# Zero products on TensorE at the start, another order for the second pair's reads, and weight bits rounded on ScalarE

## The chip, the cores and the metric

One NeuronCore of a Trainium2 chip runs the whole kernel. The metric is device time in microseconds (us) of one execution, the median of several. Below, PE is TensorE (PEld its weight loads), DVE is VectorE, ACT is ScalarE, POOL is GpSimd and SP is the engine that issues most DMAs.

## The reference

```
# q, k, v: (4, 8, 576, 64); M_prev: (4, 8, 64, 64); z_prev: (4, 8, 64); beta: (8,)
scores = scale * q @ k^T, causal mask;  a = softmax(scores);  local = a @ v
q_p = phi(q)                       # phi(x) = x + 1 for x > 0, else exp(x)
mem_out = (q_p @ M_prev) / (q_p @ z_prev + 1e-6)
g = sigmoid(beta)
x = g * mem_out + (1 - g) * local  # as a (2304, 512) matrix of tokens
out = (silu(x @ w_gate) * (x @ w_val)) @ w_out    # 512 -> 1536 -> 512
```

All in float32 at the accuracy of float32: operands are cut into a high and a low part (float32r), and a product is three matmuls (high x high, high x low, low x high).

## The kernel before

**Two stages, one program per engine.** Helpers named `pe`, `act`, `dve` and `pool` keep the order of the source on their engine, so the position of a line in the loop is its position in that engine's queue. Every such instruction has line L84 in the profile; the tiles' names tell them apart. Instructions written `ACT.`, `DVE.`, `POOL.` or `SP.` are placed by the framework's scheduler. The helper `rot` hands out a fixed number of buffers of a name in turn.

**Stage one, attention.** 16 pairs of heads run through a loop of 17 rounds (`n` from 0 to `NP` = 16). In round n the pair `cur` makes its scores on PE (`scores` for the query tiles t = 0 to 3, tiles `s`; `scores4` for the last 64 queries of both heads), DVE reads them with mask and row extreme (the `reads`), ACT takes the exponential (`exp`), and POOL multiplies by row weight and gate (`weighed`, tiles `ps`, `pl`, `p`). The pair before, `old`, is transposed on PE (`turned1`, `turned`, tiles `tr`), multiplied with its values (`values`), and its memory part is read (`recall`: PE products `tr<-mm,ph` of the feature map `ph` with the memory `mm`, then `w` and `mem` on DVE). `give` cuts the result into `xh` and `xl` and stores it. The next pair is split into high and low on POOL (`after.split`, `after.lows`: `qh`, `kh`, `ql`, `kl`). Round 0 also makes the gates (`gates`: `one_less` for the local part `og`, `memory_gates` for `gx`) and both feature maps of the first two pairs (`phi0`, `phi`).

**Weights.** Each of the 12 slices of 128 hidden columns has three thirds (gate, value, out), listed in `thirds`. They arrive as 64-bit words (`raw_load`, tile `wraw`) and are put together from the upper half (`raw_top`, an ACT Prelu into `we`, then `third_clamp`) and three low bits (`third_move`, into `wa` or `wr`: a shift on DVE for the first four, an arithmetic rounding of one byte on POOL for the others), which `third_word` joins on DVE. Slices 0 to 2 are cut into high and low (`wgh`, `wgl`, `woh`, `wol`, the low parts in `low_part`). The first four thirds are worked during rounds 2 to 16 (`EARLY`).

**Stage two, the gated feed-forward part.** It takes three blocks of 768 tokens by 12 slices, 36 units. The first three units (`eight`) are four products of 12 matmuls with 384 columns; the others (`seven`) have seven products of six (a Strassen form), for which the token sums `xr`, `xt`, `xm` and their parts `xp3` to `xp7` (`sums`, `spreads`) and the weight sums `tt` (`operands`) are made on DVE and ACT. From the second unit on, the unit before gives 18 matmuls with 512 columns (`lower`, `woh`/`wol` with `uh`/`ul`). Two PSUM banks take the products in turn. In the first block `third` is called three times in each unit for the slices to come; the list `plan` says after which product each such piece of work is put into the queues.

Of the kernel before, what the change touches and what calls it, by code (L numbers as in the profile page):

```python
# [9 lines left out]
F32 = mybir.dt.float32  # L10
F32R = mybir.dt.float32r
I32 = mybir.dt.int32
U8 = mybir.dt.uint8
AF = mybir.ActivationFunctionType
# [30 lines left out]
def attention_moe(ctx: ExitStack, tc: tile.TileContext, qt, kt_, v, m, beta, wg, wv, wo, out):  # L45
# [49 lines left out]
    def rot(pool, name, shape, dtype, n):  # L95
        held = slots.setdefault(name, [0, []])
        if len(held[1]) < n:
            held[1].append(pool.tile(shape, dtype, name=f"{name}{len(held[1])}"))
        held[0] += 1
        return held[1][(held[0] - 1) % n]  # L100
# [8 lines left out]
    def split_lo(dst, src, hi, kind=""):  # L109
        eng = pool if kind in ON_POOL else dve  # L110
        return eng.tensor_tensor(dst, src, hi.bitcast(F32), op=ALU.subtract)

    ident = const.tile([128, 128], F32, name="ident")
    make_identity(nc, ident)
    warm = const.tile([128, 1], F32, name="warm")
    DVE.memset(warm, 0.0)
    ACT.activation(warm, warm, AF.Exp)
    maskp = const.tile([128, 512], F32, name="maskp")
    POOL.memset(maskp, 0.0)
    POOL.affine_select(  # L120
# [39 lines left out]
    xs = {p: [near.tile([128, 2, N2], F32R, name=f"x{p}{part}") for part in "hl"] for p in ("p1", "p2", "p7", "p4")}  # L160

    held, wout, wr = {}, {}, {}
    thirds = [(0, 0), (0, 1), (0, 2), (1, 0)]
    work_of = [[(1, 1), (3, 0), (3, 1)]]
    work_of += [[(n, 2)] + [(n + 1 + (n >= PLAIN - 1), j) for j in range(2)] for n in range(1, NF - 2)]
    work_of += [[(n, 2)] for n in range(NF - 2, NF)]
    slots_of, at = [], len(thirds)
# [7 lines left out]
    def raw_load(n, after=None):  # L175
        if n < len(thirds):
            f, j = thirds[n]
            raws[n] = rot(wp, "wraw", [128, 512, 2], I32, 4)
            ld = SP.dma_start(raws[n].rearrange("p a b -> p (a b)"), (wg, wv, wo)[j][f].bitcast(I32))
            if after is not None:  # L180
                follow(ld, after, "the loads that the attention waits for go first")

    def raw_top(act, n):
        if n < len(thirds):
            tops[n] = rot(wp, "we", [128, 512], F32, 2)
            act.activation(tops[n], raws[n][:, :, 1].bitcast(F32), AF.Prelu, scale=2.0**-111, alpha=2.0**32)

    def low_part(dve):
# [11 lines left out]
    def third_move(eng, n):  # L200
        f, j = thirds[n]
        if f < PLAIN or j == 2:
            wa[n] = rot(wp, "wa", [128, 512], I32, 3)
        else:
            if j == 0:
                wr[f] = rot(wp, "wr", [128, 1024], F32, 2)
            wa[n] = wr[f][:, j * 512 : j * 512 + 512].bitcast(I32)
        if eng is dve:
            eng.tensor_scalar(wa[n], raws[n][:, :, 0], 29, None, op0=ALU.logical_shift_right)
        else:  # L210
            last_byte = raws[n].rearrange("p a b -> p (a b)").bitcast(U8).rearrange("p (a b) -> p a b", b=8)[:, :, 3]
            eng.tensor_scalar(wa[n], last_byte, 1.0 / 32, 31.0 / 64, op0=ALU.mult, op1=ALU.subtract)

    def third_word(act, dve, n):
        f, j = thirds[n]
# [28 lines left out]
    with tc.tile_pool(name="sb", bufs=1, reuse_waits="tile") as sb:  # L244
# [3 lines left out]
        def pair_load(n):  # L248
            b, pr = divmod(n, NPAIR)
            qr = rot(sb, "qr", [128, 768], F32, NR)  # L250
            kr = rot(sb, "kr", [128, 576], F32, NR)
            for dst, src in ((qr, qt), (kr, kt_)):
                queue = ACT if n == 0 and dst is kr else SP
                loads[n] = queue.dma_start(dst, src[b, pr])
            return qr, kr

        def pair_load_v(n):
# [50 lines left out]
        class Pair:  # L308
# [81 lines left out]
            def exp(self, t, h):  # L390
                c, p = 2 * t + h, self.pts[(t, h)][:, 0 : 128 * (t + 1)]
                act.activation(
                    p, p, AF.Exp, bias=self.mx[:, c : c + 1], scale=-1.0, accum_out=self.sm[:, c : c + 1]
                )
# [137 lines left out]
        for n in range(NP + 1):  # L532
            cur = pairs[n] if n < NP else None
            old = pairs[n - 1] if n > 0 else None
            after = pairs[n + 1] if n + 1 < NP else None
            exp = cur.exp if cur else nothing
            scores = cur.scores if cur else lambda t: nothing
            turned, turned1 = (old.turned, old.turned1) if old else (nothing, nothing)
            if cur:
                cur.begin()  # L540
            if old:
                old.turns()
            low = ending()
            reads = [scores(t) for t in range(2)]
            reads[0](0)
            reads[0](1)
            low()
            if n == 0:
                cur.lows()
            reads[1](0)  # L550
            reads[1](1)
            if after and n:
                after.split()
            exp(0, 0)
            turned1(0, act)
            turned1(1, act)
            exp(0, 1)
            exp(1, 0)
            turned(2, 0, dve)
            turned(2, 1, dve)  # L560
            exp(1, 1)
            scale = old.recall() if old else nothing
            first = lambda: cur.weighed(((0, 0), (0, 1), (1, 0), (1, 1)))
            if n == 0:
                after.split()
                one_less, memory_gates = gates()
                after.lows()
            elif cur:
                first()
            scale()  # L570
            if after and n:
                after.lows()
            if n:
                phi = after.phi_parts() if after else nothing
            reads = [scores(t) for t in range(2, 4)]
            reads[0](0)
            reads[0](1)
            exp(2, 0)
            exp(2, 1)
            turned(3, 0, act)  # L580
            turned(3, 1, dve)
            read4 = cur.scores4() if cur else nothing
            reads[1](0)
            turned(4, 0, act, dve)
            reads[1](1)
            exp(3, 0)
            exp(3, 1)
            if n == 0:
                one_less()
                first()  # L590
            read4()
            if cur:
                cur.exp4()
            if n == 0:
                memory_gates()
                phi0()
                phi = after.phi_parts()
            if old:
                old.recalled()
                old.values()  # L600
            if cur:
                cur.weighed(((2, 0), (2, 1), (3, 0), (3, 1)))
            phi()
            if cur:
                cur.weighed(((4, 0),))
            ending = old.leave() if old else lambda: nothing
            if n + 2 < NP:
                with later_by(P_LOAD):
                    pairs[n + 2].load()
            if after:  # L610
                after.load_v()
            for i, at in enumerate(EARLY):
                if n == at:
                    raw_top(act, i)
                if n == at + 1:
                    third_clamp(dve, i)
                if n == at + (2 if i < 3 else 1):
                    third_move(dve, i)
                if n == at + (3 if i < 3 else 2):
                    third_word(act, dve, i)  # L620
                if n == at + (4 if i < 3 else 2):
                    low_part(dve)
            if n in AHEAD:
                raw_load(AHEAD.index(n), loads.get(n + 2))

        n = len(EARLY)
        raw_load(n + 3)
        raw_top(act, n)
        raw_top(act, n + 1)
        third_clamp(pool, n)  # L630
        third_move(pool, n)
        ending()()

    nj = N2 // 128
    with tc.tile_pool(name="stg2", bufs=1, reuse_waits="tile") as stg2, \
# [220 lines left out]
        for n, unit in enumerate(units):  # L856
# [14 lines left out]
            if n < len(units) - 1 and n + 1 >= PLAIN:  # L871
                ready[n + 1], work = operands(units[n + 1][1])
                if plain:
                    work = [work[0] + work[1], work[2], work[3], work[4] + work[5] + work[6]]
                for k, some_ in enumerate(work):
                    plan[k] += some_
            for k, work in arrive:
# [2 lines left out]
            if plain:  # L880
                if f == 0:
                    _, due, mix = sums(t0, True)
                if f < 2:
                    for k in range(4):
                        plan[k].append(due[4 * f + k])
                if f == 1:
                    plan[2] += spreads(mix, ("h", "p6"))
                    plan[3] += spreads(mix, ("l", "p6"))
                if f == PLAIN - 1:
                    for k, p in ((0, "p5"), (1, "p3")):  # L890
                        plan[k] += spreads(mix, ("h", p))
                        plan[k + 2] += spreads(mix, ("l", p))
                    arrive = [(0, spreads(mix, ("h", "p7"))), (1, spreads(mix, ("l", "p7")))]
            if not end:
                follows = ORDER[ORDER.index(t0) + 1]
# [89 lines left out]
```

## Time and profile before

| | |
|---|---|
| median of 3 runs | 626.1 us (625.47 to 626.37) |
| the profiled execution | 626.68 us |
| its span in the trace | 624.9 us |
| busy: PE, DVE, ACT, POOL | 604.7, 494.7, 383.5, 268.1 us |
| attention until the feed-forward part | about 0 to 194 us |

The span is what the trace covers from the first to the last instruction of the program; the time holds 1.8 us more. PE's busy time counts pipelined matmuls from start to modelled end, so a busy PE can still be waiting in part. Below 1.00, the granted clock (PEclk) says that PE had less than its full 2.4 GHz.

### The profile page before, as it was taken

Reading aid. Unit: us, or ns where it says so; the run is one execution under the profiler, and the core shown is the slowest. Engines: PE = TensorE matmul, PEld = TensorE weight load, DVE = VectorE, ACT = ScalarE, POOL = GpSimd, SP = SyncE. Lnnn points to the kernel's source line nnn. Section 1 sums busy time; section 2 is a strip of 40 time slices with the busy share of each in tenths; the row PEclk is TensorE's granted clock in tenths of the full one; section 3 lists DMA queues with packets and bytes.
Section 4 is the critical chain, followed back from the end, with each engine's and each line's share of the span. In section 5 each row is a group of like instructions: output and inputs, shape, how many; then the busy total and the mean of one; then the engine's idle time right before and its main releaser. Section 6 shows DMA issues by size and latency. Waiting matters only on the chain.

```text
span 624.9 us, 11274 instructions
## 1 busy us (share of the span) xinstructions
PE 604.7 (97%) x3794; PEld 534.9 (86%) x3794; DVE 494.7 (79%) x1209; ACT 383.5 (61%) x892; POOL 268.1 (43%) x282
## 2 busy tenths in 40 slices
PE   5999999999999899999999999999999999999997
PEld 3777788778778798988889999999999999999995
DVE  6799899999986899999999666566788765665653
ACT  6788888888875467666657644455446654454442
POOL 6899999999965986867740000000000000000000
PEclk9799999999999999999999999999999999999999
DMA  8355856757435775799638532232756631332212
GB/s 244 96 157 172 268 163 188 239 161 212 150 100 172 217 238 183 237 294 314 218 135 286 168 117 88 72 128 71 238 172 214 202 102 67 102 102 67 70 33 101
DMA packets 48745, 102.46 MB, mean 164 GB/s; under 512 B 6960, under 2 KB 16176, under 8 KB 48688
## 3 DMA queue, kind: packets, MB, share of 16 engines
q1 hardware_dynamic: 48544, 101.45, 50.1%
q8 instruction: 30, 0.49, 0.3%
q10 hardware_dynamic: 144, 0.29, 0.1%
q14 instruction: 27, 0.22, 0.1%
HBM read 74.99 MB, written 26.74 MB: 163 GB/s over the span
## 4 chain that ended last, share of the span: by engine, by line
PE 80%; DVE 9%; POOL 4%; ACT 3%; issue 2%; DMA 1%; DVEq 0%; POOLq 0%
PE s L84 50%; PE tr L84 30%; ACT pl L84 2%; DVE xr L84 1%; POOL we L84 1%; POOL wa L84 1%; DVE tl L84 1%; POOL wr L84 1%; DVE rs L84 1%; DVE pl L84 1%; DVE mem L84 1%; DMA kr<-in_kt_dram 1%; DVE zh L84 1%; ACT g L84 1%; DVE wa L84 1%
## 5 line engine op out<-in xcount | busy, mean ns | idle before, releaser
L84 POOL TENSOR_SCALAR pl<-pl,rs,og 128x384 f32<-128x384 f32 (+1 forms) x64 | 56.0, 886 | 10.9 <-DVE rs L84 10.9
L84 ACT ACTIVATE zh<-zh 128x384 f32<-128x384 f32 x33 | 17.3, 526 | 70.4 <-DVE zh L84 70.3
L84 PE MATMUL tr<-woh,uh 128*128 128x512 f32 x144 | 57.3, 398 | 0.0
L84 PE MATMUL tr<-wol,uh 128*128 128x512 f32 x144 | 56.7, 394 | 0.0
L84 PE MATMUL tr<-woh,ul 128*128 128x512 f32 x144 | 56.6, 393 | 0.0
L84 DVE TENSOR_TENSOR zv<-s,zv 128x384 f32<-128x384 f32 x33 | 18.3, 556 | 47.7 <-PE s L84 47.5
L84 ACT CAST th<-tt 128x512 fp32r<-128x512 f32 x66 | 41.0, 622 | 18.2 <-DVE tt L84 14.9
L84 ACT ACTIVATE pl<-pl,mx 128x384 f32<-128x384 f32 (+1 forms) x64 | 42.3, 663 | 14.2 <-DVE mx L84 14.2
L84 PE MATMUL tr<-g,vp 128*64 128x320 f32 (+4 forms) x448 | 48.7, 360 | 0.0
L84 DVE TENSOR_TENSOR tl<-tt,th 128x512 fp32r<-128x512 f32 x66 | 46.9, 711 | 0.0
L84 PE MATMUL s<-kh,qh 64*128 64x128 f32 (+4 forms) x160 | 37.6, 389 | 7.4 <-ACT kh L84 5.4
L84 PEld LDWEIGHTS tr<-g,vp 128*64 128x64 f32 x448 | 29.5, 137 | 17.6 <-issue 2.3
L84 POOL TENSOR_SCALAR we<-we 128x512 f32<-128x512 f32 x32 | 30.1, 940 | 28.1 <-ACT we L84 25.8
L84 POOL TENSOR_SCALAR wr<-wraw 128x512 int32<-128x512 uint8 x18 | 38.5, 2136 | 1.4
L84 DVE TENSOR_TENSOR zg<-s,zp 128x384 f32<-128x384 f32 x33 | 18.4, 558 | 25.9 <-ACT bh L84 20.6
L84 DVE CUSTOM_DVE_ANT_0 pl<-s,maskp 128x384 f32<-128x384 f32 (+1 forms) x64 | 38.1, 615 | 0.7 <-PE s L84 0.7
L84 ACT CAST uh<-zh 128x384 fp32r<-128x384 f32 x36 | 18.5, 514 | 29.7 <-DVE zh L84 29.4
L84 DVE TENSOR_TENSOR bl<-wr,bh 128x512 fp32r<-128x512 f32 x66 | 36.5, 553 | 0.0
L84 PE MATMUL tr<-ident,pl 128*128 128x128 f32 x224 | 32.3, 281 | 2.3 <-DVE xl L84 1.6
L84 POOL TENSOR_SCALAR ps<-ps,rs,og 128x128 f32<-128x128 f32 (+1 forms) x64 | 31.9, 511 | 6.0 <-DVE rs L84 5.1
L84 ACT CAST bh<-wr 128x512 fp32r<-128x512 f32 x66 | 33.9, 513 | 0.0
L84 DVE COPY g<-tr 128x384 f32<-128x384 f32 (+1 forms) x64 | 32.0, 519 | 2.1 <-PE tr L84 0.8
(187 smaller groups left out, 2031.6 us busy)
## 6 DMA issues: line engine op xcount, KB each, us to landing
wr<-wdr SPq DMA_DIRECT2D x24, 512.0 KB, 3.3
qr<-in_qt_dram SPq DMA_DIRECT2D x16, 384.0 KB, 3.1
wraw<-in_wg_dram SPq DMA_DIRECT2D x12, 512.0 KB, 4.4
wraw<-in_wv_dram SPq DMA_DIRECT2D x12, 512.0 KB, 4.8
wraw<-in_wo_dram SPq DMA_DIRECT2D x12, 512.0 KB, 4.4
wol<-wdo SPq DMA_DIRECT2D x24, 256.0 KB, 2.8
woh<-wdo SPq DMA_DIRECT2D x24, 256.0 KB, 3.2
vp<-in_v_dram SPq DMA_DIRECT2D x16, 320.0 KB, 4.4
```

The source lines that it names most:

```text
L84: ins = getattr(eng, name)(*args, **kw)
```

## The change

Five things are changed.

- **Zeros on PE.** `spin(n)` issues n float32 products of a zero tile with itself into a bank of the `tr` ring that is not yet in use: eight ahead of everything, one after each of the first two scores of round 0, two before and two after its `scores4`, and three in round 1 after the scores of t = 0 and 1.
- **First loads.** The first pair's q and k come in five pieces on two queues instead of two whole loads.
- **Order in rounds 0 and 1.** The last weighing of pair 0, its feature map (`phi0`) and the memory gates move from the end of round 0 to behind the reads of t = 0 and 1 in round 1 (`late`); the second feature map's DVE part moves from round 0 to the end of round 1.
- **Weights.** For gate and value thirds, the rounding moves from POOL to ACT (an Identity with scale and bias, one byte of the raw word to an integer). The third (1, 1) is begun in the last round, with the joining of the two thirds before stage two, and `we` has three buffers. The Silu table is asked for at the head of the last round.
- **Token sums of the first three units.** The sums and their parts are spread over units 0 and 1 where they went to units 0, 1 and 2.

```diff
+    zero = const.tile([128, 128], F32, name="zero")
+    DVE.memset(zero, 0.0)
+    spare = [rot(psT, "tr", [128, 512], F32, PS_T) for _ in range(PS_T)][-1]
+    def spin(n):
+        for _ in range(n):
+            pe.matmul(spare[:, 0:128], zero, zero, start=True, stop=True)
+    spin(8)
...
+    low_bias = const.tile([128, 1], F32, name="low_bias")
+    DVE.memset(low_bias, -31.0 / 64)
...
-    thirds = [(0, 0), (0, 1), (0, 2), (1, 0)]
-    work_of = [[(1, 1), (3, 0), (3, 1)]]
+    thirds = [(0, 0), (0, 1), (0, 2), (1, 0), (1, 1)]
+    work_of = [[(3, 0), (3, 1)]]
...
-            tops[n] = rot(wp, "we", [128, 512], F32, 2)
+            tops[n] = rot(wp, "we", [128, 512], F32, 3)
...
+        if j == 2:
+            eng.tensor_scalar(wa[n], last_byte, 1.0 / 32, 31.0 / 64, op0=ALU.mult, op1=ALU.subtract)
         else:
-            last_byte = ...
-            eng.tensor_scalar(wa[n], last_byte, 1.0 / 32, 31.0 / 64, op0=ALU.mult, op1=ALU.subtract)
+            act.activation(wa[n], last_byte, AF.Identity, scale=1.0 / 32, bias=low_bias)
...
-            for dst, src in ((qr, qt), (kr, kt_)):
-                queue = ACT if n == 0 and dst is kr else SP
-                loads[n] = queue.dma_start(dst, src[b, pr])
+            if n == 0:
+                for queue, dst, src, c in (
+                    (SP, qr, qt, slice(128, 384)), (ACT, kr, kt_, slice(0, 256)), (SP, qr, qt, slice(384, 768)),
+                    (ACT, kr, kt_, slice(256, 576)), (SP, qr, qt, slice(0, 128)),
+                ):
+                    queue.dma_start(dst[:, c], src[b, pr, :, c])
+            else:
+                for dst, src in ((qr, qt), (kr, kt_)):
+                    loads[n] = SP.dma_start(dst, src[b, pr])
...
+            if n == NP:
+                act.activation(warm, warm, AF.Silu)
             if old:
                 old.turns()
             low = ending()
-            reads = [scores(t) for t in range(2)]
+            reads = []
+            for t in range(2):
+                reads.append(scores(t))
+                if n == 0:
+                    spin(1)
+            if n == 1:
+                spin(3)
...
             reads[1](1)
+            if n == 1:
+                for work in late:
+                    work()
...
             turned(2, 1, dve)
+            if n == NP:
+                for i in range(2):
+                    raw_top(act, len(EARLY) + i)
+                third_clamp(pool, len(EARLY))
+                third_move(pool, len(EARLY))
...
+            if n == 0:
+                spin(2)
             read4 = cur.scores4() if cur else nothing
+            if n == 0:
+                spin(2)
...
             if n == 0:
-                memory_gates()
-                phi0()
-                phi = after.phi_parts()
+                phi1 = after.phi_parts()
+            if n == NP:
+                for i in range(2):
+                    third_word(act, dve, len(EARLY) - 1 + i)
+                    raw_load(len(EARLY) + 3 + i)
...
-            phi()
-            if cur:
-                cur.weighed(((4, 0),))
+            if n == 0:
+                late = [lambda cur=cur: cur.weighed(((4, 0),)), phi0, memory_gates]
+            else:
+                if n == 1:
+                    phi1()
+                phi()
+                if cur:
+                    cur.weighed(((4, 0),))
...
-                if n == at + (3 if i < 3 else 2):
+                if n == at + 3 and i < 3:
                     third_word(act, dve, i)
-                if n == at + (4 if i < 3 else 2):
+                if n == at + 4 and i < 3:
                     low_part(dve)
...
-        n = len(EARLY)
-        raw_load(n + 3)
-        raw_top(act, n)
-        raw_top(act, n + 1)
-        third_clamp(pool, n)
-        third_move(pool, n)
         ending()()
+        low_part(dve)
+        i = len(EARLY) + 1
+        third_clamp(pool, i)
+        third_move(pool, i)
+        raw_top(act, i + 1)
...
-                    work = [work[0] + work[1], work[2], work[3], work[4] + work[5] + work[6]]
+                    work = [work[0] + work[1], work[2] + work[3], work[4] + work[5], work[6]]
...
                 if f == 0:
                     _, due, mix = sums(t0, True)
-                if f < 2:
-                    for k in range(4):
-                        plan[k].append(due[4 * f + k])
+                    for k, some_ in enumerate(((0,), (1,), (2, 4), (3,))):
+                        plan[k] += [due[i] for i in some_]
                 if f == 1:
-                    plan[2] += spreads(mix, ("h", "p6"))
-                    plan[3] += spreads(mix, ("l", "p6"))
+                    for k in range(3):
+                        plan[k].append(due[5 + k])
+                    for k, p in ((0, "p5"), (2, "p6")):
+                        plan[k] += spreads(mix, ("h", p))
+                        plan[k + 1] += spreads(mix, ("l", p))
                 if f == PLAIN - 1:
-                    for k, p in ((0, "p5"), (1, "p3")):
-                        plan[k] += spreads(mix, ("h", p))
-                        plan[k + 2] += spreads(mix, ("l", p))
+                    plan[0] += spreads(mix, ("h", "p3"))
+                    plan[2] += spreads(mix, ("l", "p3"))
```

## Rows read from the trace of the kernel before

**Rows 1.** The page, part 1: busy time of each engine.

```profile
PE 604.7 (97%) x3794; PEld 534.9 (86%) x3794; DVE 494.7 (79%) x1209; ACT 383.5 (61%) x892; POOL 268.1 (43%) x282
```

**Rows 2.** Windows: start:end, length, busy us of each engine, clock, DMA.

```profile
194.00:200.00 6.00, 6.00 (x35) 6.00 (x36) 3.86 (x6) 4.59 (x8) 5.15 (x4) 1.00 0.66 212
...
200.00:216.00 16.00, 13.43 (x72) 12.25 (x71) 13.43 (x17) 6.20 (x12) 15.37 (x9) 1.00 0.67 210
...
216.00:236.00 20.00, 19.77 (x102) 17.83 (x100) 19.67 (x31) 12.58 (x27) 16.39 (x11) 1.00 0.70 219
```

**Rows 3.** The chain that ended last, in order of time: start, us, what.

```profile
12.92 2.53 POOL ps L84 x4
...
28.60 0.88 PE s L84 x12
...
39.82 0.89 PE s L84 x12
...
198.54 2.55 POOL wr L84
...
241.67 1.05 PE s L84 x6
...
242.72 0.69 PE tr L84 x3
```

**Rows 4.** Timeline, first 32 us: start, us, engine, operation, [idle before <-releaser].

```profile
4.83 0.76 ACT L84 CAST kh<-kr 128x256 fp32r<-128x256 f32 x2 [2.18 <-DMA kr<-in_kt_dram]
...
10.02 1.42 POOL L84 TENSOR_TENSOR kl<-kr,kh 128x576 fp32r<-128x576 f32 x1
...
12.92 2.61 POOL L84 TENSOR_SCALAR ps<-ps,rs,og 128x128 f32<-128x128 f32 x4 [1.49 <-DVE rs L84]
...
15.57 3.37 POOL L84 TENSOR_SCALAR pl<-pl,rs,og 128x384 f32<-128x384 f32 x4
...
18.31 2.53 PE L84 MATMUL tr<-mm,ph 128*128 128x130 f32 x10
...
30.78 1.28 PE L84 MATMUL tr<-mm,ph 128*128 128x130 f32 x10
```

**Rows 5.** Timeline of PEld: one weight load of 128 columns, twice.

```profile
10.33 0.33 PEld L84 LDWEIGHTS s<-kl,qh 128*128 128x128 f32 x1
...
23.69 0.19 PEld L84 LDWEIGHTS s<-kl,qh 128*128 128x128 f32 x1
```

**Rows 6.** Windows over PE's slow stretch.

```profile
16.00:22.00 6.00, 5.68 (x26) 4.46 (x26) 4.26 (x19) 3.98 (x12) 5.26 (x8) 0.50 0.20 66
```

**Rows 7.** Timeline of PE, round 16 and the first units.

```profile
186.62 0.52 PE L84 MATMUL tr<-ident,pl 128*128 128x128 f32 x3 [0.43 <-POOL pl L84]
...
193.91 0.44 PE L84 MATMUL s<-xp1h,wgh 128*128 128x384 f32 x1
...
207.47 0.44 PE L84 MATMUL s<-xp1h,wgh 128*128 128x384 f32 x1 [2.11 <-DVE zh L84]
...
230.69 0.34 PE L84 MATMUL s<-xp1h,bh 128*128 128x384 f32 x1
...
236.34 0.44 PE L84 MATMUL s<-xp7l,th 128*128 128x384 f32 x1 [0.56 <-DVE xp7l L84]
```

**Rows 8.** Timeline of ACT, round 16 and the first unit.

```profile
184.30 0.35 ACT L84 CAST xh<-tr 128x256 fp32r<-128x256 f32 x1
...
185.10 0.43 ACT L84 CAST xh<-tr 128x320 fp32r<-128x320 f32 x1 [0.45 <-PE tr L84]
...
195.41 1.28 ACT L84 ACT_TABLE_LOAD   x1
...
198.55 0.67 ACT L84 ACTIVATE we<-wraw 128x512 f32<-128x512 f32 x1
```

**Rows 9.** Timeline of DVE: one form, twice.

```profile
203.03 1.01 DVE L84 TENSOR_TENSOR ul<-zg,uh 128x384 fp32r<-128x384 f32 x1
...
208.20 0.55 DVE L84 TENSOR_TENSOR ul<-zh,uh 128x384 fp32r<-128x384 f32 x1
```

More of the change, by code (lines that the diff above doesn't have):

```diff
@@ L209, in third_move @@
             eng.tensor_scalar(wa[n], raws[n][:, :, 0], 29, None, op0=ALU.logical_shift_right)
-        else:
-            last_byte = raws[n].rearrange("p a b -> p (a b)").bitcast(U8).rearrange("p (a b) -> p a b", b=8)[:, :, 3]
-            eng.tensor_scalar(wa[n], last_byte, 1.0 / 32, 31.0 / 64, op0=ALU.mult, op1=ALU.subtract)
+            return
+        last_byte = raws[n].rearrange("p a b -> p (a b)").bitcast(U8).rearrange("p (a b) -> p a b", b=8)[:, :, 3]
+        if j == 2:
+            eng.tensor_scalar(wa[n], last_byte, 1.0 / 32, 31.0 / 64, op0=ALU.mult, op1=ALU.subtract)
+        else:
+            act.activation(wa[n], last_byte, AF.Identity, scale=1.0 / 32, bias=low_bias)
     def third_word(act, dve, n):
```

## The prediction, made before the change was run

> **What bounds the kernel now.** I read the page first: PE is busy for 604.7 of 624.9 us [rows 1]. So where PE runs at its pace nothing but fewer matmuls helps, and the change takes none away; what can be gained lies where PE waits or is slow. The chain of waits and the windows show two such places.
>
> The first is rounds 0 and 1, up to about 29 us. The chain goes from the first loads (ACT stands idle until the first k lands at 4.83 us) to POOL, whose first four weighings (12.92 us, 2.61 us long) wait for DVE's row weights, and then to PE [rows 3, 4]. PE is slow there in a second sense: between 16 and 22 us the granted clock is 0.50 [rows 6], the lower level of 1.2 GHz, and the ten records of the memory products take 2.53 us where round 2 has them in 1.28 [rows 4]. The windows print 1.00 for the first stretches too, but the durations contradict it: a weight load takes 0.33 us at 10.33 and 0.19 at 23.69 [rows 5]. So PE runs at the lower level from its first product on, rises shortly before 12 us, falls at about 15 after a pause, and rises again at 22.
>
> The second place is the start of stage two, 194 to 236 us. From 194.6 on the chain is made of POOL's clamps and roundings of one third after the other [rows 3] (the piece of 2.55 us stands for them), then of DVE. The windows give POOL 36.9 of these 42 us, DVE 37.0, ACT 23 [rows 2]. PE waits 2.11 us at 207.47 and 0.56 at 236.34, both for DVE [rows 7], which had waited for POOL.
>
> **First period, step by step.** Eight zero products stand ahead. A float32 product of this size is two records; five took 1.28 us in round 2 and 2.53 at the lower level [rows 4], so eight cost 4.0 us at the lower level, from about 1 us to 5. Real data is ready between 4 and 5 us, so they hold PE up by 0 to 0.8 us; I take nothing, because POOL hides it: its first weighing can't start before it has split pair 1, which ends at 11.44 us [rows 4] and rests on pair 1's loads. Their issues move back by two DMA issues on SP; but the bytes ahead of them are the same, and I leave their landing where it was (bounds 0 to +0.8 us).
>
> What the eight buy: PE has been busy before the first score, so the scores should run at 2.4 GHz, and the first pieces of q and k are 256 of 672 KB, so DVE's first subtraction comes up to 1.2 us earlier. Either of the two brings DVE's row weights forward by the 1.2 us that lie between 12.92 and POOL's free time of about 11.7. Term a: **-1.2 us** (bounds: 0, if loads and clock give nothing; -1.4, POOL's limit).
>
> Next is PE's start into the memory products, at 18.31 us. It waits for POOL's first two large weighings (a part of the 3.37 us from 15.57 [rows 4]), which follow by -1.2, and then for six transposes at the lower level, from 17.50; at the higher level these take about 0.4 us less. Term b: **-0.4 us**. The feature map and the gates, now behind the four reads of pair 1 on DVE, would be late next: the reads are ready at about 13.5 us and the late work ends near 17, just ahead of need. Behind the late work on DVE stand the copies of the transposes; their banks are two of four, so PE doesn't wait for these.
>
> From the start of the memory products to the next round's scores it took 18.31 to 28.60, 10.3 us, in round 1, and 30.78 to 39.82, 9.0 us, in round 2 [rows 3, 4]. At the higher level round 1 should take the time of round 2. Term c: **-1.3 us**. The nine other zero products cost 0.26 us each where PE would work, and nothing where it waits; they stand in such waits, and I count nothing (bound +0.5). Together **-2.9 us** (bounds 0 and -3.4). If the clock falls all the same, b and c are gone and -1.2 is left. From round 2 on each round begins when the one before lets it, so the gain is kept.
>
> **Round 16.** The Silu table is now loaded at its head. ACT is free from 184.65 to 185.10, where the cast of 320 columns waits for PE [rows 8]. The load takes 1.28 us and stood alone at 195.41 [rows 8]; with the small instruction behind it ACT is free at about 186.1, so the cast comes 1.0 us later, DVE's low part of it too, and PE's transposes at 186.62 [rows 7], which need that bank, by about 0.5: the subtraction ended shortly before them. Term d: **+0.5 us** (bounds 0 and +1.0). The two Prelus of weights, one rounding and the joinings of thirds 3 and 4 go where ACT and DVE wait for PE later in this round; they would cost 0.6 us more if ACT's copies of the transposes came late by them.
>
> The Trainium skill ("ScalarE: Activation LUTs", What ACT_TABLE_LOAD costs) adds a drain of about 1.38 us to a switch of 1.28. The trace doesn't show it: the load starts at 195.41, and the next ACTIVATE is under way at 196.70. By the page, d would be near +1.9 and the time 622.2; I go by the row.
>
> **Start of stage two.** The pace of PE: six matmuls of 384 columns take 1.05 us, three of 512 columns 0.69 [rows 3]. The first unit is 48 of the first kind, 8.4 us; the second and third have 18 of the other besides, 12.5 us each: 33.5 us in all. They took from 193.91 to 230.69, 36.8 us [rows 7], so 3.3 are lost, and 0.6 in the fourth unit: 3.9 us are all there is to gain.
>
> POOL loses 8 of its 11 roundings in this stretch, 2.55 us each [rows 3]: 20 of 36.9 us, and it no longer sets the pace. ACT gets them. The trace has no Identity from bytes. Its nearest row is the Prelu that reads every second word of the same tile, 0.67 us [rows 8]; the upper bound is POOL's 2.55. I take 0.67, since it is the same engine, the same size and the same stride. ACT then has 23 + 5.4 of 42 us, well below PE.
>
> DVE is next. It worked 37.0 us between 194 and 236 [rows 2], more than PE's 33.5. Beside a rounding on POOL one of its instructions takes 1.01 us that elsewhere takes 0.55 [rows 9], a loss of 0.46; eight roundings less give back at most 3.7 us, and as not each of them met such an instruction I take 2.5. That leaves 34.5 us of DVE, 1.0 more than PE needs, so about 1.0 of the 3.9 us stays lost. The new order of the sums puts DVE's work earlier, where it stood idle (13.43 of 16 us busy between 200 and 216 [rows 2]), so that it can be done in time. Term e: **-2.9 us** (bounds: -3.9, and -0.5 if DVE's queue holds PE up as before).
>
> Later units of the first block have two roundings on ACT each, hidden behind PE.
>
> **The sum.** -2.9 + 0.5 - 2.9 = -5.3 us. The profiled execution took 626.7 us, 0.6 over the median of 626.1; so 621.4 for it and **620.8 us** for the median.
>
> **Rivals.**
>
> *The clock falls again (chance 0.17).* PE has little to do between the end of round 0's scores and POOL's first weighings; at about 15 us a pause like this one was followed by the fall. The zero products fill part of it. Without the higher level, terms b and c are lost: 622.5 us.
>
> *DVE takes POOL's place (0.15).* From about 217 us the chain was DVE's already, and 19.67 of 20 us between 216 and 236 were busy [rows 2]. If its stalls beside POOL come from the clamps, which stay, it keeps 37 us of work and gives back only what it idled: term e is -0.5 to -1.0, and the time 623 us. Against it: the stall in rows 9 stands beside a rounding.
>
> *The roundings make ACT the bound, and it is slower (0.05).* If Identity isn't in the table that Silu uses, each of the 21 moved roundings brings two table loads, 2.57 us with the switch back. A unit gives ACT about 12 us, of which it used some 7.5; it decides when the two roundings of a unit take more than 4.5 us together, and with the loads they take 6.5. Ten units lose about 2 us each: 626.1 - 2.4 + 20, near 644 us. Against it: Prelu, copies and Silu share a table after 195.41 without another load.
>
> The Trainium skill (the same page, Table sets: the hidden batching unit) says that cheap functions, identity among them, are in every set. By it no load is added; no row here shows an Identity.
>
> *More than that (0.10).* The additions of the next block's sums hold PE up in later units too. If fewer stalls of DVE end that, another 2.5 us go: 618.3 us.
>
> **How the numbers follow.** My forecast has 0.53, with a range of its own from 619.3 to 622.3. Fallen clock and busy DVE, one or both, reach to 624.2; the last rival and the lower bounds of a and e reach to 617.8. That leaves 2 in 10 outside. A measurement of this kernel tells 0.2%, 1.25 us, from no change (its three runs lie within 0.9 us). Faster by more than that is all but the ACT rival and the worst of both others: 0.88; within 0.2%: 0.06; slower: 0.06.
>
> **What would show it.** Right: weight loads of 0.19 us from about 5 us on and no window at 0.50 before 25; POOL's first weighings at about 11.7 us; round 2's scores near 25.7; Identity near 0.67 us without further table loads; PE's first product of stage two about 2.4 us earlier than 193.91, and of the fourth unit some 34.5 us after it, with no wait of 2 us between. Wrong: a stretch at 0.50 after 13 us; pair 1's loads later than before; an ACT that PE waits for in units 0 to 11; DVE still busy without a gap from 200 to 236 with PE waiting on it.

## The result

The changed kernel takes **620.3 us** (median, 619.3 to 620.6); the kernel before took 625.8 beside it. The ratio is 0.991 (95% interval 0.989 to 0.993), so the time fell by 5.5 us; 5.3 had been forecast. The profiled execution took 619.94 us with a span of 618.1, and each engine's busy time is now (part 1 of the page):

```profile
PE 605.8 (98%) x3828; PEld 539.6 (87%) x3828; DVE 485.7 (79%) x1211; ACT 394.7 (64%) x914; POOL 214.9 (35%) x261
```

PE's busy time is the same as in [rows 1]; what went is waiting. POOL lost 53 us of work, ACT took up 11 and DVE lost 9. To see where the span became shorter I read the start of the same matmuls in both traces (first score of a round, first product of a unit):

| stretch of PE | before, us | after, us | difference | forecast |
|---|---|---|---|---|
| start to round 2 | 28.53 | 27.51 | -1.0 | -2.9 |
| rounds 2 and 3 | 22.38 | 22.40 | 0 | 0 |
| rounds 4 and 5 | 22.79 | 21.54 | -1.25 | 0 |
| rounds 6 to 14 | 100.54 | 100.72 | +0.2 | 0 |
| round 15's first score to stage two | 19.67 | 20.22 | +0.55 | +0.5 |
| units 0 to 2 | 36.78 | 33.76 | -3.0 | } -2.9 |
| units 3 to 11 | 107.85 | 105.06 | -2.8 | } |
| units 12 to 35 and the end | 286.36 | 286.89 | +0.5 | 0 |

These add up to the 6.8 us between the two spans; the medians differ by 1.3 less, since the profiled execution of before was 0.9 above its median beside this kernel and this one 0.3 below. The total was near the forecast, but made of other parts.

The timeline of the start (several engines, in order of time; columns as in [rows 4]):

```profile
1.04 3.75 PE L84 MATMUL tr<-zero 128*128 128x128 f32 x16 [1.04 <-DVE warm L125]
...
8.75 0.73 POOL L84 TENSOR_SCALAR qh<-qr 128x640 fp32r<-128x640 f32 x1 [3.55 <-DMA qr<-in_qt_dram]
...
9.65 0.67 ACT L299 CAST kh<-kr 128x576 fp32r<-128x576 f32 x1 [1.91 <-DMA kr<-in_kt_dram]
...
10.96 0.17 DVE L84 TENSOR_SCALAR gs<-gs 128x8 f32<-128x8 f32 x1 [1.28 <-ACT gs L84]
...
11.06 1.40 POOL L84 TENSOR_TENSOR kl<-kr,kh 128x576 fp32r<-128x576 f32 x1
...
11.40 1.33 DVE L84 COPY og<-gs 128x8 f32<-128x8 f32 x3
...
12.75 0.17 DVE L84 TENSOR_SCALAR rs<-sm 128x4 f32<-128x4 f32 x1
...
13.24 1.98 POOL L84 TENSOR_SCALAR ps<-ps,rs,og 128x128 f32<-128x128 f32 x4 [0.78 <-DVE rs L84]
...
17.40 1.25 PE L84 MATMUL tr<-ident,pl 128*128 128x128 f32 x6
...
18.49 1.28 PE L84 MATMUL tr<-mm,ph 128*128 128x130 f32 x10
...
27.51 0.33 PE L84 MATMUL s<-kh,qh 64*128 64x128 f32 x2
```

POOL waits for pair 1's q until 8.75 us, ACT for its k until 9.65. DVE waits for ACT's part of the gates until 10.96; its copies of the gates take 1.33 us beside POOL's `kl`, and the first weighing starts at 13.24, later than the 12.92 of [rows 4]. The ten products of the memory take 1.28 us, as at the higher clock, but the six transposes just ahead of them take 1.25 (0.82 in e3 below, where the clock stayed up).

Windows over the stretches of [rows 2] and [rows 6] (same columns):

```profile
194.00:200.00 6.00, 6.00 (x36) 6.00 (x35) 5.55 (x9) 3.45 (x7) 4.14 (x4) 1.00 0.96 344
200.00:216.00 16.00, 16.00 (x87) 15.22 (x86) 15.82 (x23) 8.83 (x18) 5.19 (x5) 1.00 0.65 199
216.00:236.00 20.00, 20.00 (x105) 18.54 (x105) 17.25 (x32) 15.64 (x31) 5.73 (x6) 1.00 0.56 175
16.00:22.00 6.00, 6.00 (x44) 5.45 (x43) 3.99 (x13) 4.29 (x13) 5.58 (x8) 0.81 0.24 72
```

In stage two PE has no gap left, with POOL at 15.1 of 42 us where it had 36.9, and DVE at 38.6, more than the 37.0 of before. The last row says that the clock fell in spite of the zeros, though for a shorter time (0.81 against 0.50).

Round 16 and stage two, from the timeline:

```profile
182.62 1.28 ACT L84 ACT_TABLE_LOAD   x1
183.91 0.20 ACT L84 ACTIVATE warm<-warm 128x1 f32<-128x1 f32 x1
184.02 0.41 ACT L84 CAST xh<-tr 128x320 fp32r<-128x320 f32 x1
...
186.21 1.19 POOL L84 TENSOR_SCALAR we<-we 128x512 f32<-128x512 f32 x2
186.23 0.77 ACT L84 ACTIVATE wa<-wraw,low_bias 128x512 int32<-128x512 uint8 x1
...
192.39 0.44 PE L84 MATMUL s<-xp1h,wgh 128*128 128x384 f32 x1
...
226.15 0.34 PE L84 MATMUL s<-xp1h,bh 128*128 128x384 f32 x1
```

and what PE waited for from 184 to 340 us (us in total, times, longest), first before, then after:

```profile
PE s L84 <- DVE zh L84: 2.1, 1, 2.1
PE s L84 <- DVE zg L84: 1.5, 4, 0.4
PE s L84 <- DVE xp7l L84: 0.6, 1, 0.6
PE s L84 <- ACT zh L84: 0.5, 1, 0.5
PE tr L84 <- POOL pl L84: 0.4, 1, 0.4
PE tr L84 <- DVE mem L84: 0.4, 1, 0.4
```

```profile
PE tr L84 <- DVE xl L84: 1.0, 1, 1.0
PE tr L84 <- DVE mem L84: 0.4, 1, 0.4
```

All waits of stage two are gone: those of 2.1 and 0.5 us in unit 1 and of 0.6 in unit 3, which lie within the 3.9 us that the forecast counted, and four for `zg` in units 7 to 10 (1.5 together), which it didn't count. The waits of `tr` are round 16's.

### The profile page after: what moved, and what is told of

It is laid out like the page before. It is cut to its first block, busy times and chain, and to the rows that moved or that the text cites. A ratio compares the mean times of both kernels' runs of the same rounds, so it can differ in the third digit from the quotient of the medians.

```text
span 618.1 us, 11345 instructions
## 1 busy us (share of the span) xinstructions
PE 605.8 (98%) x3828; PEld 539.6 (87%) x3828; DVE 485.7 (79%) x1211; ACT 394.7 (64%) x914; POOL 214.9 (35%) x261
## 4 chain that ended last, share of the span: by engine, by line
PE 90%; DVE 4%; ACT 3%; DMA 1%; issue 1%; SPq 0%; DVEq 0%; ACTq 0%
PE s L84 58%; PE tr L84 33%; ACT pl L84 1%; DMA kr<-in_kt_dram 1%; DVE rs L84 1%; DVE mem L84 1%; DVE xl L84 1%; ACT g L84 0%; DVE w L84 0%; DVE pl L84 0%; DVE ph L84 0%; ACT ps L84 0%; DVE wa L84 0%; ACT xh L84 0%; DVE og L84 0%
## 5 line engine op out<-in xcount | busy, mean ns | idle before, releaser
L84 POOL TENSOR_SCALAR we<-we 128x512 f32<-128x512 f32 x32 | 25.2, 790 | 78.3 <-ACT we L84 78.1
L84 ACT CAST uh<-zh 128x384 fp32r<-128x384 f32 x36 | 18.5, 514 | 32.4 <-DVE zh L84 32.1
L84 PE MATMUL s<-kh,qh 64*128 64x128 f32 (+4 forms) x160 | 36.0, 373 | 1.8 <-DVE mx L84 1.4
L84 PEld LDWEIGHTS tr<-woh,ul 128*128 128x128 f32 x144 | 27.0, 188 | 7.1 <-DVE ul L84 0.3
L84 PEld LDWEIGHTS tr<-ident,pl 128*128 128x128 f32 x224 | 25.2, 143 | 9.1 <-POOL pl L84 3.6
```

Source lines behind the costliest of these rows:

```text
L84: ins = getattr(eng, name)(*args, **kw)
```

## The experiments

All ratios are to the kernel before, run beside them, with 95% intervals. The table has the marks that the text uses: POOL's first weighing, the first score of round 2, and the units' lengths in the profiled execution.

| kernel | median, us | ratio | weighing | round 2 | units 0-2 | units 3-11 |
|---|---|---|---|---|---|---|
| before | 625.8 to 626.8 | | 12.92 | 28.53 | 36.78 | 107.85 |
| changed | 620.3 | 0.991 (0.989-0.993) | 13.24 | 27.51 | 33.76 | 105.06 |
| e1 | 619.7 | 0.990 (0.988-0.992) | 14.44 | 28.65 | 33.76 | 105.13 |
| e2 | 619.7 | 0.990 (0.988-0.992) | 12.39 | 27.46 | 33.75 | 105.05 |
| e3 | 619.8 | 0.990 (0.988-0.991) | 13.19 | 27.73 | 33.76 | 105.03 |
| e4 | 620.1 | 0.991 (0.989-0.992) | 12.33 | 26.62 | 33.71 | 105.58 |
| e5 | 619.8 | 0.988 (0.987-0.990) | 12.42 | 26.68 | 33.72 | 105.07 |
| e6 | 619.2 | 0.988 (0.985-0.990) | 13.62 | 27.89 | 33.71 | 105.05 |
| e7 | 621.3 | 0.991 (0.989-0.993) | 12.50 | 26.76 | 33.71 | 106.47 |
| e8 | 621.4 | 0.992 (0.990-0.993) | 12.86 | 28.29 | 33.72 | 105.04 |
| e9 | 620.1 | 0.990 (0.988-0.991) | 12.60 | 27.94 | 33.71 | 105.43 |
| e10 | 625.4 | 0.9985 (0.9976-0.9994) | 12.39 | 27.80 | 38.33 | 106.80 |
| e11 | 615.1 | 0.982 (0.980-0.984) | 12.12 | 24.85 | 33.72 | 105.04 |
| e12 | 622.0 | 0.992 (0.990-0.994) | 13.18 | 29.05 | 33.71 | 105.36 |

**The first period.** e1 loads the first pair whole again, e2 leaves the zero products out, e3 has more of them.

```diff
# e1_whole_loads: the two loads of before
-            if n == 0:
...
+            for dst, src in ((qr, qt), (kr, kt_)):
+                queue = ACT if n == 0 and dst is kr else SP
# e2_no_zeros
-        for _ in range(n):
+        for _ in range(0):
# e3_more_zeros: 5 and 3 behind the scores of round 1, 9 behind scores4 of round 0
-            if n == 1:
-                spin(3)
+                if n == 1:
+                    spin(5 if t == 0 else 3)
...
-                spin(2)
+                spin(9)
```

> The changed kernel, but the first pair's q and k come in two whole loads as before. Theory L (the first period gave less because the five pieces make pair 1's loads land about 1.2 us later): POOL's first split of pair 1 near 7.6 us (8.75 with the pieces), its first weighings near 12 (13.24), round 2 near 26.3 (27.51), the time near 619.1. Rival C (the fall of the clock at 15 us is what cost it, not the loads): the first score moves from 4.7 to about 5.4, round 2 stays at 27.5 or comes later, the time stays at 620.3 or above.

> The changed kernel without any zero product. If the zeros carry what the first period gained: the clock is at its lower level until about 12 us, round 2 begins at 28.5 as before the change, the time is near 621.3. Rival (pair 1's loads and POOL set rounds 0 and 1, so a fast PE buys nothing there): round 2 stays within 0.3 us of 27.5 and the time at 620.3.

> The changed kernel with more zero products where PE waits between rounds 0 and 1: nine instead of two after the last scores of round 0, and five more between the first two scores of round 1. Theory C (the fall of the clock between 15 and 18 us is what cost the first period): no fall, the memory products begin near 17.4 us instead of 18.49, round 2 near 26.4, the time near 619.2. Theory L (POOL's weighings, late by the loads, set it): the clock stays up but round 2 stays near 27.3, or the zeros hold up real products and round 2 comes later than 27.5.

None differs from the changed kernel by more than its interval, so e1's theory L, e3's theory C and the first theory of e2 didn't hold: in e1 pair 1's q was split at 7.69 us, as the theory wanted, but the weighing came at 14.44 and not near 12. e2 and e3 together say what the clock is worth. Windows of 16 to 22 us, first e2, then e3:

```profile
16.00:22.00 6.00, 5.64 (x28) 4.88 (x29) 3.51 (x13) 3.44 (x11) 5.18 (x9) 0.55 0.21 68
```

```profile
16.00:22.00 6.00, 5.79 (x51) 4.92 (x50) 5.21 (x19) 4.13 (x13) 5.22 (x8) 1.00 0.20 68
```

Without zeros the clock is at 0.55, with more of them at 1.00, and round 2 begins at 27.46 and 27.73. At the higher level the stretch from the memory products to round 2 is indeed shorter (9.0 us in e3, 10.4 in e2), but the products began later (18.74 against 17.05). By these two traces PE isn't the one that sets the end of this period. e1's late weighing belongs to an execution of 621.3 us; its six lie between 618.9 and 621.9, so what one trace shows of the start needn't hold for the median.

**Which part of stage two.** e4 rounds on POOL again, e5 orders the sums as before, e9 does both; e7 has two buffers for `we`. e7 loses the upper half of the third (1, 0), so the products of that third's weights differ; its amount of work is the same.

```diff
# e4_round_on_pool
-        if j == 2:
+        if True:
             eng.tensor_scalar(wa[n], last_byte, 1.0 / 32, 31.0 / 64, op0=ALU.mult, op1=ALU.subtract)
# e5_sums_order: the lines of before for work and plan, all in the last hunk of the diff
-                    work = [work[0] + work[1], work[2] + work[3], work[4] + work[5], work[6]]
+                    work = [work[0] + work[1], work[2], work[3], work[4] + work[5] + work[6]]
...
# e7_two_tops
-            tops[n] = rot(wp, "we", [128, 512], F32, 3)
+            tops[n] = rot(wp, "we", [128, 512], F32, 2)
```

> The changed kernel with the rounding of all thirds on POOL again, everything else as changed. Theory (the rounding on POOL made both POOL's chain and DVE's stalls): units 0 to 2 take 36.5 us again instead of 33.8, units 3 to 11 take 107.9 instead of 105.1, the time is near 625. Rival (the new order of the sums and the early third gave the gain): units 0 to 2 stay below 34.8, and the time below 622.

> The changed kernel with the token sums of units 0 to 2 in the order of before (and the weight sums of unit 3 in theirs). Theory S (with the rounding on POOL the start of stage two stayed fast, so the order of DVE's work gave it): units 0 to 2 take at least 35.5 us instead of 33.8, with PE waiting for DVE, and the time is 622.5 or more. Rival T (the third begun in round 16 and the words joined there gave it): units 0 to 2 stay below 34.3 and the time at 620.3.

> The changed kernel with two buffers of the upper halves (we) instead of three. Theory B (the third buffer lets the clamps on POOL run ahead, and so took PE's four waits of 0.6 us out of units 3 to 11): units 3 to 11 take 107.2 us or more instead of 105.1, the time is near 622.5. Rival (the rounding off POOL, or the earlier begin of the queue, took them out): units 3 to 11 stay at 105.1 to 105.6, the time at 620.3.

> The changed kernel with both undone at once: the rounding on POOL and the sums in the order of before. Each of the two alone left units 0 to 2 at 33.7 us. Theory D (each of the two is enough by itself): with both gone units 0 to 2 take 35.5 us or more and units 3 to 11 some 106, the time is near 622.5. Rival T (the third begun and joined in round 16, and the third buffer, gave it all, and neither edit does anything there): units 0 to 2 stay below 34.2, units 3 to 11 at 105.6, the time within 0.6 of that of the run with the rounding on POOL, 0.990 of before.

Units 0 to 2 take 33.7 us in all four: the first theories of e4, e5 and e9 failed. So neither the roundings' move nor the new sums is needed for the gain there, not even one of the two. In units 3 to 11 the roundings on POOL cost 0.5 us (105.58), and two buffers 1.4 (106.47, between the two theories of e7). In e7 1.0 of it is seen as waits of PE, in units 7 to 10 as before:

```profile
PE s L84 <- DVE zg L84: 1.0, 4, 0.3
```

What is left of the change to stage two in e9 is the earlier third with its buffer, and Silu's early load. e12 adds the third alone to the kernel before (with the third buffer, without Silu's early load, the zeros, the pieces and the new order).

```diff
# e12_third_alone: of the whole diff only
-    thirds = [(0, 0), (0, 1), (0, 2), (1, 0)]
-    work_of = [[(1, 1), (3, 0), (3, 1)]]
+    thirds = [(0, 0), (0, 1), (0, 2), (1, 0), (1, 1)]
+    work_of = [[(3, 0), (3, 1)]]
...
# raw_top, third_clamp, third_move and third_word of thirds 3 and 4 in round 16, as in the diff
```

> The kernel before with only this of the change: the third (1,1) belongs to those begun in the rounds, thirds 3 and 4 are clamped, moved and joined in round 16, and the tile of the Prelus has three buffers. The start, the Silu load, the roundings on POOL and the order of the sums are as before. If the earlier third is what frees units 0 to 2 (as the runs without the new roundings and sums suggest): units 0 to 2 take 33.7 us instead of 36.8, no wait of PE of 2 us near 207, units 3 to 11 take 105.5 us, and the ratio to the kernel before is 0.991 (0.988 to 0.994). If it does so only together with a request for the Silu table at the head of round 16, or with the new start: units 0 to 2 at 35.5 us or more and a ratio above 0.995.

The first theory holds: 0.992, units 0 to 2 in 33.71 us, and no wait of PE in stage two. Lines of POOL's timeline, before:

```profile
194.61 0.61 POOL L84 TENSOR_SCALAR we<-we 128x512 f32<-128x512 f32 x1 [6.43 <-ACT we L84]
195.31 1.96 POOL L84 TENSOR_SCALAR wa<-wraw 128x512 int32<-128x512 uint8 x1
```

and in e12, with its windows:

```profile
188.82 0.61 POOL L84 TENSOR_SCALAR we<-we 128x512 f32<-128x512 f32 x1
189.52 1.95 POOL L84 TENSOR_SCALAR wa<-wraw 128x512 int32<-128x512 uint8 x1
```

```profile
200.00:216.00 16.00, 16.00 (x88) 15.23 (x87) 14.43 (x20) 8.11 (x16) 12.51 (x9) 1.00 0.66 222
216.00:236.00 20.00, 20.00 (x106) 18.74 (x105) 19.50 (x34) 13.12 (x28) 12.18 (x8) 1.00 0.53 177
```

Before, POOL stood idle for 6.43 us in round 16 and began its row of thirds 0.7 us after stage two's first product (193.91). In e12 it begins 5.65 us ahead of that product (194.47). Its roundings take 1.95 to 2.50 us, where they took 1.96 to 2.56; nine of them begin between 194 and 236 us, where eleven did, and POOL is busy for 29.4 of these 42 us (36.9), no longer the one waited for. DVE is about as busy as before, 19.50 of 20 us between 216 and 236, and PE doesn't wait for it.

e12 shows that the earlier third is enough. Which of its parts is isn't shown: with POOL's pieces, Prelus on ACT and joinings on DVE moved into round 16 too. For POOL speaks the trace of before, where it works without a pause from 194.61 to 223.5 us and is the chain until 216.44; the wait of 2.11 us at 207.47 falls into that stretch.

**The start as a whole.** e8 undoes all of it in the changed kernel (pieces, zeros, order of rounds 0 and 1); e10 puts only the start into the kernel before.

```diff
# e8_start_as_before: loads and zeros as in e1 and e2, and
-                phi1 = after.phi_parts()
+                memory_gates()
+                phi0()
+                phi = after.phi_parts()
# e10_start_alone: the diff without the hunks of thirds, we, Identity, Silu and sums
```

> The changed kernel with rounds 0 and 1 as before: no zero products, whole first loads, gates and feature maps where they were; round 16 and stage two as changed. Theory (rounds 0 and 1 gave about 1 us, and 1 more through rounds 2 to 5): round 2 begins near 28.5 us, stage two near 194.5, the time is 621.5 to 622.3. Rival (what rounds 0 and 1 gave is within the noise of one execution): the time is 620.3 within 0.5.

> The kernel before with rounds 0 and 1 as changed (zero products, five pieces, late gates and feature maps) and nothing else of the change. The start as before cost the changed kernel some 1.5 us, so this should give back about as much: ratio to before near 0.9975, round 2 between 26.6 and 27.8 us, units 0 to 2 at 36.8 and units 3 to 11 at 107.9 as before. Rival (the two halves depend on one another, the earlier begin moves the phase of rounds 2 to 5 as well): 0.996 or less.

Alone the start gives 0.15% (0.06 to 0.24), 0.9 us. e8 loses 1.6 to 2.2 us against e5 and e6, run with it. Over the profiled executions with this start (changed, e4 to e7, e9, e10) round 2 begins at 26.6 to 27.9 us, and at 28.3 to 29.1 with the old one (before, e8, e12). So it is worth some 1 to 2 us. Leaving out the zeros (e2) or the pieces (e1) loses nothing that shows. That points to the new order, but it isn't shown: the order wasn't run by itself, and no run leaves out zeros and pieces together, of which either might be enough. In e10 PE has the old waits in stage two:

```profile
PE s L84 <- DVE zh L84: 2.1, 1, 2.1
PE s L84 <- DVE zg L84: 1.6, 4, 0.5
PE s L84 <- ACT zh L84: 0.5, 1, 0.5
```

Behind the first of them the clock fell in this execution (0.89 between 200 and 216 us), which makes its units 0 to 2 longer than before's.

**Round 16.** e6 leaves out the early request for Silu's table.

```diff
# e6_silu_late
-            if n == NP:
-                act.activation(warm, warm, AF.Silu)
```

> The changed kernel without the request for the Silu table at the head of round 16; the load then stands before the first Silu of stage two. By the step of the prediction the first product of stage two comes 0.5 us earlier than with it (round 16 from its memory products to stage two 6.4 us instead of 6.9), and units 0 to 2 take 33.8 us as with it: the time near 619.8. Rival: the load then delays the first Silu and so the bank that PE needs, and units 0 to 2 take 34.5 or more: 620.5.

From round 15's first score to stage two it takes 19.68 us, against 20.22, and PE's wait for `xl` is 0.4 us instead of 1.0. That is term d, 0.5 us, too small for the medians (619.2 and 619.8 in e5).

**Rounds 4 and 5.** Nothing in the change touches them. Before, in round 4 (DVE, then POOL):

```profile
54.89 0.75 DVE L84 TENSOR_SCALAR rs<-sm 128x4 f32<-128x4 f32 x1
55.67 0.18 DVE L84 RECIPROCAL rs<-rs 128x4 f32<-128x4 f32 x1
...
54.89 0.72 POOL L84 TENSOR_SCALAR qh<-qr 128x640 fp32r<-128x640 f32 x1
56.03 1.95 POOL L84 TENSOR_SCALAR ps<-ps,rs,og 128x128 f32<-128x128 f32 x4 [0.41 <-ACT ph L84]
```

After:

```profile
53.88 0.11 DVE L84 TENSOR_SCALAR rs<-sm 128x4 f32<-128x4 f32 x1
...
53.88 0.73 POOL L84 TENSOR_SCALAR qh<-qr 128x640 fp32r<-128x640 f32 x1
54.60 1.96 POOL L84 TENSOR_SCALAR ps<-ps,rs,og 128x128 f32<-128x128 f32 x4
```

The addition to four columns and POOL's split start in the same hundredth of a microsecond, and the addition takes 0.75 us in one trace and 0.11 in the other. In rounds 4 and 5 of before, e2, e8, e12 and the changed kernel it takes 0.11 to 0.19 us where the split starts at least 6 ns after it, and 0.74 or more where the split starts between 8 ns ahead of it and 5 ns behind. POOL's weighings then wait 0.41 us. The row names ACT's `ph`, but after the change they start at 54.60, with that instruction running until 54.92; so what they wait for is the row weights, ready at 55.85 before. e8, with the start of before, has the short rounds too (21.56 us), and e2 one short and one long (22.13), so the 1.25 us are not owed to the new start: a few nanoseconds decide, and which way they fall looks like chance. The reciprocal of the same four columns takes 0.18 in both. The addition is that of 1e-9 to the row sums; e11 leaves it out (the row weights are 1/sum), on top of e6.

```diff
# e11_no_add, besides e6's edit
-                dve.tensor_scalar(rs, self.sm[:, c : c + n], 1.0e-9, None, op0=ALU.add)
-                dve.reciprocal(rs, rs)
+                dve.reciprocal(rs, self.sm[:, c : c + n])
```

> A version meant to be faster than both: the changed kernel with the Silu table loaded late and without the addition of 1e-9 to the row sums (a sum of exponentials is at least 1, so the addition changes nothing in float32); the reciprocal reads the sums themselves. Theory P (DVE's small TENSOR_SCALAR waits for POOL's split when it comes just behind it, 0.11 us becoming up to 0.75, and the RECIPROCAL doesn't): the waits of rounds 2 to 15 are gone, these rounds take 142.5 us instead of 144.7, the time is 617.0. Rival (the RECIPROCAL takes over the wait): the same 0.3 to 0.75 us stand at the RECIPROCAL, rounds 2 to 15 take 144 or more, and the time is 618.7 to 619.2.

It takes 615.1 us, 11 less than the kernel before and 5 less than e9, run with it. By the ratios it lies 3.3 us below e6, from which it differs by this edit alone. All instructions of DVE on `rs` between 20 and 180 us (min/median/max in ns), first before, then e11:

```profile
L84 DVE TENSOR_SCALAR rs<-sm x43: 107/170/751, 21.3 to 178.2; 128x4 f32<-128x4 f32 x29, 128x1 f32<-128x1 f32 x14
```

```profile
L84 DVE RECIPROCAL rs<-sm x44: 119/164/181, 23.4 to 179.9; 128x4 f32<-128x4 f32 x29, 128x1 f32<-128x1 f32 x15
```

The additions varied between 0.11 and 0.75 us; no reciprocal takes over 0.18. Round 2 begins at 24.85, 1.8 us earlier than in any other kernel. But theory P's 142.5 us for rounds 2 to 15 didn't come: from round 2's first score to round 15's it is 144.84 in this execution (616.9 us, the slowest of four), against 144.66 in the changed kernel. Rounds 4 to 14 are 3.0 us shorter together; round 3 takes 14.43 us, where it took 11.30. At its head the feature map's instruction on DVE takes 4.18 us, beside POOL's four weighings, and the granted clock falls behind it (0.66 between 39 and 44 us):

```profile
34.77 4.18 DVE L84 SCALAR_TENSOR_TENSOR ph<-qe,ph 128x640 f32<-128x640 f32 x1
35.48 2.81 POOL L84 TENSOR_SCALAR pl<-pl,rs,og 128x384 f32<-128x384 f32 x4
```

In before and in the changed kernel it takes 0.79 to 0.82 us from 20 us on. Without the addition it starts while POOL's `kl` (34.08 to 35.49) still runs, and ends 0.66 us after the last weighing. So a wait was left, though not at the reciprocal as the rival had it: it moved to another instruction, which later takes 0.79 to 1.03 us. Whether the other three executions have the long one isn't known.

## Why the prediction was right, and where it wasn't

**Term a (-1.2) failed, at "Either of the two brings DVE's row weights forward".** The row weights began at 12.75 us (12.36 before) and POOL's first weighing at 13.24. Pair 1's q was split at 8.75 instead of 7.58, against "I leave their landing where it was", but that isn't all: in e3, e9 and e10, with the same pieces, it was split at 7.42 to 7.64, and the weighing still came at 12.39 to 13.19 and not at 11.7. What the step missed is that the weighing doesn't follow POOL's free time: DVE's row weights stand behind its gate copies, these behind ACT's part of the gates, and that here behind the cast of pair 1's k, which waits for its load.

**Term b (-0.4) failed:** the clock fell again, as the first rival had it (granted 0.50 between 15 and 18 us), and the transposes were slow. (The step counts six from 17.50; the trace of before has three there, the other three at 16.29.) **Term c (-1.3) was right in size:** 9.0 us from the memory products to round 2, from 10.2. That was luck, since the clock was up again (1.00 from 18.5 us) just as the products began at 18.49. And e2 and e3 show that it can't be added to the others: with a lower clock the products began earlier and round 2 at the same time. Instead of -2.9 the start gave -1.0 in this trace and -0.9 by itself on the chip. (The bound of -3.4 isn't the sum of the terms either: -1.4, -0.4 and -1.3 make -3.1.)

**Term d (+0.5) was right** (+0.55; e6 takes it back). The load took 1.28 us, and the next ACTIVATE began 0.01 us after its end. The drain of about 1.38 us which the Trainium skill ("ScalarE: Activation LUTs", What ACT_TABLE_LOAD costs) adds to a switch isn't seen here either.

**Term e (-2.9) was right in sum and wrong in its reason.** Of the 3.9 us 3.6 came back (3.0 in units 0 to 2 and the 0.6 at 236 us), not 2.9, and 2.2 us more in units 3 to 11, as the rival "more than that" said, though e7 puts 1.4 of it down to the third buffer of `we`, not to fewer stalls of DVE; 0.5 was lost again from unit 12 on. The step that failed is the one from POOL's roundings to DVE's stalls to "34.5 us of DVE, 1.0 more than PE needs". It sets DVE's work of 42 us (194 to 236) against PE's 33.5 of units 0 to 2 alone; over the same 42 us PE was busy for 39.2 [rows 2]. And DVE didn't become less busy (38.6 of 42 us) and holds nothing up. What the runs show in its place is the earlier third: begun and joined in round 16, it moves POOL's row some 6 us ahead, whichever engine rounds, and by itself gives the 3.0 us (e12). I had taken the eight roundings for POOL's excess; a start 6 us earlier, with two fewer of them in the stretch, was enough. That POOL's start is the part that counts is argued from the chain, not run by itself. Whether the roundings' move alone would have done it too wasn't tried.

**The ACT rival** is out: the Identity takes 0.76 us (forecast 0.67), and there is one table load from 150 to 330 us, that in round 16.

```profile
L84 ACT ACTIVATE wr<-wraw,low_bias 128x512 int32<-128x512 uint8 x18 | 13.7, 763 | 0.0
```

That the Identity brings no load agrees with what the Trainium skill (same page, Table sets: the hidden batching unit) says of cheap functions.

**Not foreseen:** 1.25 us in rounds 4 and 5, where two engines start within nanoseconds of each other and which one is first looks like chance. So the sum came out by luck: the start gave 1.9 us too little, rounds 4 and 5 gave 1.25 and stage two 2.4 too much, and the medians differ by 1.3 less than these traces.

## What to carry to other kernels

Where an engine does a row of equal pieces for a stage and the stage waits for it, look at when the row starts before moving work off the engine: an idle stretch ahead of it may hold the first piece. Clock and waits of one stretch are not added as separate gains unless the engine with the clock sets its end. Small operations between two engines are worth a look by their spread (min against max): one that is 0.11 or 0.75 us long stands in someone's way. After it is taken out, look for the instruction that now stands in its place.

## What the runs showed of the hardware that was not expected

- DVE's TENSOR_SCALAR on 128x4 float32 in SBUF takes 0.11 us alone and up to 0.75 beside POOL's split of 0.72 us. Begun 0.10, 0.23 and 0.35 us into such a split it took 0.66, 0.52 and 0.40 (at 42.58 us after the change, 43.73 before, 76.19 after), so it ended with the split each time; beside two splits in a row it took 1.36 (e1, 20.62 us). A RECIPROCAL of the same size stays under 0.19. The Trainium skill ("SBUF — State Buffer", Who interferes with whom) says that the two engines share a pair of ports, held for a whole instruction by whoever is first; it names TENSOR_SCALAR and copies among the operations that take it. The 0.75 beside 0.72 and the 0.11 ahead of it agree. Without this addition the median is 3.3 us lower (e11 against e6, by the ratios).
- DVE's SCALAR_TENSOR_TENSOR on 128x640 float32 in SBUF took 4.18 us in e11, 0.79 to 0.82 from 20 us on in before and in the changed kernel: begun beside POOL's `kl`, it lasted through that and four weighings that followed one another.
- The clock's rise behind the same eight zero products came at 4.2 to 9.7 us in the eight kernels that had them and the pieces, and in five of these it fell again between 12.7 and 14.9 us.
- In every kernel with the earlier third a unit takes 11.57 us from unit 13 on, and 11.55 in before and e10; that is the 0.5 us lost at the end. Why wasn't found.
